# An attention and gated-convolution kernel: q and k loaded alike for both row groups, v issued sooner, reciprocal broadcasts and the first normalisations one to two steps later

## The chip, the cores and the metric

The kernel runs on one core of a Trainium2 chip. The metric is the device time of one execution in microseconds; three runs of the kernel before gave 496.06 us as median (496.01 to 496.46).

## The reference

For four batches of 576 tokens and eight heads of width 64, `q` and `k` are rotated, and softmax attention is computed per head. The heads of a token are laid side by side (512 wide), go through a 512 to 1024 matrix with a ReLU, a convolution of three taps along the tokens, a sigmoid gate, and a 1024 to 512 matrix.

```python
def rotate(x):                      # cos, sin: 576 x 32
    x1, x2 = (x[..., :half], x[..., half:])
    return np.concatenate([x1 * cos - x2 * sin, x1 * sin + x2 * cos], axis=-1)
scores = scale * np.matmul(rotate(q), rotate(k).transpose(0, 1, 3, 2))
attn = np.exp(scores - np.max(scores, axis=-1, keepdims=True))
attn = attn / (np.sum(attn, axis=-1, keepdims=True) + 1e-09)
x = np.matmul(attn, v)              # heads side by side: (4, 576, 512)
h = np.maximum(x @ w_in, 0.0)
conv_out[:, t] = sum(conv_w[k] * h[:, t + k - 1] for k in range(3))
out = (h * sigmoid(conv_out)) @ w_out
```

The weights arrive as 64-bit floats and are turned into 32-bit ones on the chip.

## The kernel before

The work is cut into 16 pairs of heads, p = 0 to 15 (four per batch), and each pair into five steps of 128 query rows (the last has 64). Step number m = 5p + s sets nearly everything: a table `plan` holds for each step a list of pieces with a rank, and `emit` writes the pieces out in order of step and rank. The engines get their instructions in just that order, and each engine runs its own in order, so an instruction that waits holds up all behind it on its engine.

For a pair the pieces are these. `load` (L141 to L151) brings q or k from memory, two heads, in blocks of 32 tokens, into one buffer each (`rq`, `rk`). Each head fills two groups of 32 partitions: the first group gets the row of 64 numbers as it is, in one transfer; the second gets it with its halves swapped, in two. `rope` (L186) rotates on GpSimd (POOL) by six multiplications with the table `tabt` and three additions; `emit_TQ` (L230) turns the result on VectorE (DVE) into `qT` or `kT`, from where TensorE (PE) reads it. `emit_S` makes the scores on TensorE (`sp`), the maxima on VectorE (`negm`) and the exponentials on ScalarE (`st`, and `sums`). `emit_T` transposes them on TensorE (`tp`), ScalarE copies them to `pt`. `emit_E` (L382) multiplies by v (`vm`, `vr`) into `xn`. `emit_rinv` (L363) makes the reciprocals of the sums, writes them to memory in four small transfers (`rd`), and reads them back in three transfers, spread over 64 partitions each (`rb`). The function `norm` (L401) multiplies `xn` by `rb`, and for the first blocks the result goes by DMA to `xT` (L413).

Up to step 25 the kernel is in its first phase, which also converts the weights (`wt`, `wf`: four VectorE instructions a piece, L593 to L609). From step 26 (`WIDE`) on, the two big matrices (`emit_M1`, which reads `xT`, L443; `emit_M2`, `m2_half`) run beside the attention of later pairs, and after the last pair alone.

What matters for the loads: `rq` and `rk` have one buffer each, so the load of pair p waits for `emit_TQ` of pair p - 1. All loads but a few at the start are issued by SyncE (SP), whose queue also holds `rd`, `rb`, `xT`, the loads of v and of the weights (L629), and copies of converted weights (`winl`, L662). Eight completion counters go round, so that a transfer on this queue can be issued only when the one that used its counter last has landed.

Of the kernel before, what the change touches and what calls it, by code (L numbers as in the profile page):

```python
# [20 lines left out]
def attention_moe_kernel(ctx, tc, q, k, v, w_in, conv_w, w_out, tab, tabx, out):  # L21
    nc = tc.nc
# [119 lines left out]
    def load(p, part):  # L142
        b, hp = divmod(p, NPB)
        x = raw[p, part] = p1.tile([128, S // 32, 2, 32], F32, tag="r" + part, name="r" + part)
        for h in range(2):
            y = (q if part == "q" else k)[b, 2 * hp + h].rearrange("(c i) d -> i c d", i=32)
            r0 = slice(64 * h, 64 * h + 32)
            r1 = slice(64 * h + 32, 64 * h + 64)
            nc.sync.dma_start(out=x[r0].rearrange("i c e d -> i c (e d)"), in_=y)
            nc.sync.dma_start(out=x[r1, :, 0, :], in_=y[:, :, 32:64])  # L150
            nc.sync.dma_start(out=x[r1, :, 1, :], in_=y[:, :, 0:32])  # L151

    vmain = {}

    def load_v(p):
        if p < 2:
            nc.vector.memset(vrem[p], 0.0)
        b, hp = divmod(p, NPB)
        t = vmain[p] = p1.tile([128, 2, 4, D], F32, tag="vm", name="vm", bufs=2)
        for h in range(2):  # L160
            nc.sync.dma_start(out=t[:, h], in_=v[b, 2 * hp + h, 0:512, :].rearrange("(t p) d -> p t d", p=128))
            nc.sync.dma_start(out=vrem[p % 2][64 * h:64 * h + 64, h, :], in_=v[b, 2 * hp + h, 512:S, :])
# [23 lines left out]
    def rope(p, part):  # L186
        x = raw[p, part]
        for a in range(0, 18, 3):
            y = x[:, a:a + 3]
            nc.gpsimd.tensor_tensor(out=y, in0=y, in1=tabt[:, a:a + 3], op=ALU.mult)  # L190
        for a in range(0, 18, 6):
            y = x[:, a:a + 6]
            nc.gpsimd.tensor_tensor(out=y[:, :, 0, :], in0=y[:, :, 0, :], in1=y[:, :, 1, :], op=ALU.add)
# [36 lines left out]
    def emit_TQ(p, part):  # L230
        qk_tiles(p)
        x = raw.pop((p, part))[:, :, 0, :]
        if part == "q":
            nc.vector.transpose(out=QT[p].rearrange("p (c i) -> p c i", i=32), in_=x)
        else:
            kt = KT[p].rearrange("p (c i) -> p c i", i=32)
            nc.vector.transpose(out=kt[:, 2:20], in_=x)  # L237
            if p * STEPS < WIDE:
                for h in range(2):
                    r = slice(64 * h, 64 * h + 64)  # L240
                    nc.vector.transpose(out=krem[p % 2][r, r].rearrange("p (c i) -> p c i", i=32), in_=x[r, 16:18])
            if p * STEPS + STEPS > WIDE:
                nc.vector.transpose(out=kt[:, 0:2], in_=x[:, 16:18])
# [6 lines left out]
    def go(d, key):  # L250
        for fn in d.pop(key):
            fn()
# [106 lines left out]
            at(late["n"], 5 if late["n"] > WIDE else 11, lambda dst=dst[:, i], ps=ps: evac("A", dst, ps))  # L359

    rb = {}

    def emit_rinv(p):  # L363
        rv = rvc[p % 2]
        rt = p1.tile([128, 32], F32, tag="rt", name="rt")
        nc.vector.tensor_scalar(out=rv[:, 0:9], in0=sums[p], scalar1=1e-9, scalar2=None, op0=ALU.add)
        nc.vector.reciprocal(out=rv[:, 0:9], in_=rv[:, 0:9])
        nc.vector.transpose(out=rt, in_=rv)
        d = scr.tile([9, 128], F32, tag="d", name="rd")
        for i in range(0, 128, 32):  # L370
            nc.sync.dma_start(out=d[:, i:i + 32], in_=rt[i:i + 9, :])
        fl = d.rearrange("(o t) n -> o (t n)", o=1)
        rbt = rb[p] = p1.tile([128, S], F32, tag="rb", name="rb")
        nc.sync.dma_start(out=rbt[0:64, :], in_=fl[:, 0:S].to_broadcast([64, S]))
        nc.sync.dma_start(out=rbt[64:128, 0:512], in_=fl[:, 640:1152].to_broadcast([64, 512]))
        nc.sync.dma_start(out=rbt[64:128, 512:S], in_=fl[:, 576:640].to_broadcast([64, 64]))
# [330 lines left out]
    WIDE = 26  # L707
    UNITS = {n: 1 for n in (26, 27, 28, 29, 31, 32, 33, 34)}
    UNITS.update({n: 2 for n in (36, 38, 41, 43, 46, 48, 51, 53, 56, 58, 61, 63, 66, 69, 71, 74, 77, 79)})
    HALVES = [37, 39, 42, 44, 47, 49, 52, 54, 57, 59, 62, 64, 67, 68, 72, 73, 76, 78]  # L710
    NORM = {4: 8}
    SPLIT = (38, 39, 42, 43, 44, 45, 47, 48)
    LATEW = (
# [8 lines left out]
    def at(n, rank, fn):  # L722
        plan.setdefault(n, []).append((rank, len(plan.get(n, [])), fn))

    def emit():
        with tc.manual_schedule(engines=engines):
# [6 lines left out]
            for part in "qrk":  # L733
                emit_TQ0(part)
            nc.sync.dma_start(out=tabt, in_=tabx.rearrange("p (c e d) -> p c e d", e=2, d=32))
            load(1, "q")
            load_w(0)
            emit_S(0, 0)
            load(1, "k")
            load_w(1)  # L740
            load_v(0)
# [3 lines left out]
            for p in range(1, NP):  # L745
                n = STEPS * p
                early = n - 10 >= WIDE - 1
                for i, part in enumerate("qk"):
                    if p > 1:
                        at(max(n - 10, WIDE) if early else n - 9 + 2 * i, 19.6 if early else 19, lambda p=p, part=part: load(p, part))  # L750
                    at(n - 8 + i if early else max(n - 6, 0), 18, lambda p=p, part=part: rope(p, part))
                    at(n - 5 + i * (n - 15 < WIDE) if early else max(n - 4 + 2 * i, 2), 0.45, lambda p=p, part=part: emit_TQ(p, part))
                at(n + 1, 19, lambda p=p: load_v(p))
            for p in range(NP):
                n = STEPS * p
                for s in range(STEPS):
                    m = n + s
                    first = m < WIDE
                    if m:
                        at(m - 1 if first else m, 0.5 if first else 0, lambda p=p, s=s: emit_S(p, s))  # L760
                    at(m, 0.2, lambda p=p, s=s: go(reds, (p, s)))
                    at(m, 0.3 if first else 1.5, lambda p=p, s=s: go(exps, (p, s)))
                    for h in range(2 if s < 4 else 1):
                        at(m + 1, 0 if m + 1 < WIDE else 1, lambda p=p, s=s, h=h: emit_T(p, s, h))
                if n + 4 < WIDE:
                    for i in range(4):
                        at(n + 1 + i, 2, lambda p=p, i=i: emit_Trem(p, i))
                else:
                    for i in range(4):
                        at(n + 1 + i, 1.1, lambda p=p, i=i: emit_Trem(p, i))  # L770
                if n + 8 < WIDE:
                    for i in range(4):
                        at(n + 5 + i, 4, lambda p=p, i=i: emit_E(p, i // 2, XW // 2 * (i % 2), XW // 2))
                else:
                    for i in range(2):
                        m = n + 5 + (i if n + 5 < WIDE else 0)
                        at(m, 4 if m < WIDE else 10, lambda p=p, i=i: emit_E(p, i))
                at(n + 5, 4.5, lambda p=p: emit_rinv(p))
                for j in range(2):
                    at(n + NORM.get(p, 8 if n + 8 < WIDE else 7) + (j if p <= WIDE // STEPS else 0), 1.7 + j, lambda p=p, j=j: norms.pop((p, j))())  # L780
            whole, done = sum(c for c, _ in wsteps), 0
# [21 lines left out]
            n = -1  # L803
            while any(plan.values()):
# [17 lines left out]
                while plan.get(n):  # L822
                    e = min(plan[n], key=lambda e: e[:2])
# [16 lines left out]
            t = HS * last // 128  # L840
# [11 lines left out]
def _tables(S, D):  # L852
    import numpy as np

    half = D // 2
    inv_freq = 1.0 / 10000.0 ** (np.arange(0, half, dtype=np.float32) / half)
    fr = np.outer(np.arange(S, dtype=np.float32), inv_freq)
    res = []
    for f in (np.cos(fr), np.sin(fr)):
        f = np.asarray(f, np.float32)  # L860
        m = f[:512].reshape(4, 128, 1, half).transpose(1, 0, 2, 3)
        res.append(np.ascontiguousarray(np.broadcast_to(m, (128, 4, 2, half)).reshape(128, 8, half)))
        r = np.concatenate([f[512:], f[512:]], 0).reshape(128, 1, half)
        res.append(np.ascontiguousarray(np.broadcast_to(r, (128, 2, half))))
    parts = [res[0], res[2], res[1], res[3], np.eye(128, dtype=np.float32)]
    root = float(D) ** -0.25
    cs = [(root * np.cos(fr)).astype(np.float32), (root * np.sin(fr)).astype(np.float32)]
    cs = [x.reshape(S // 32, 32, half).transpose(1, 0, 2) for x in cs]
    turned = [np.stack([cs[0], x], axis=2) for x in (-cs[1], cs[1])]
    return {  # L870
        "tab": np.ascontiguousarray(np.concatenate([x.reshape(128, -1) for x in parts], axis=1)),
        "tabx": np.ascontiguousarray(np.concatenate(turned * 2, axis=0).reshape(128, -1)),
    }
# [26 lines left out]
```

## Time and profile before

| What | Value |
|---|---|
| Median of three runs | 496.06 us (496.01 to 496.46) |
| The profiled execution's own time | 498.59 us |
| Span from its first to its last instruction | 496.7 us |
| PE, DVE, ACT, POOL busy | 460.5, 353.7, 328.3, 291.3 us |
| Mean granted TensorE clock | 0.983 |
| DMA read and written | 37.12 and 4.79 MB |

The times of this section's table and of all rows below are of the one profiled execution. A row's "idle" is the engine's idle time just before an instruction, and the name behind the arrow is what ended it, as far as semaphores show it. Busy time of TensorE is no measure of its speed, since matmuls are pipelined and their ends are modelled. The order listings below the diff are the built programs' order on one engine, with no time in them.

### The profile page before, as it was taken

To read this page: it belongs to the slowest core of one execution; us is meant where nothing else is said; L and a number is where in the kernel's file an instruction comes from. 1 tells how busy PE (TensorE), PEld (TensorE's weight loads), DVE (VectorE), ACT (ScalarE), POOL (GpSimd) and SP (SyncE) were. 2 spreads that over 40 slices of the span, in tenths; PEclk is the share of its full clock that TensorE was granted. 3 is DMA by queue.
4 is the path that set the end of the run, shared out by engine and by line. 5 is a ranking of instruction groups with operands and counts; after the bars stand their busy time and mean duration, and the time that the engine had idled before them with its cause. 6 is when DMAs were issued, how large, how long until landed. Compare 5 with 4: busy or idle time off the path is not lost.

```text
span 496.7 us, 12280 instructions
## 1 busy us (share of the span) xinstructions
PE 460.5 (93%) x4508; PEld 355.3 (72%) x4508; DVE 353.7 (71%) x640; ACT 328.3 (66%) x943; POOL 291.3 (59%) x479
## 2 busy tenths in 40 slices
PE   1888878788999999999999999999999999999997
PEld 1355545455667587777778797979797878899986
DVE  5597695886689988667867777777675565467931
ACT  2687675777698878686859696868687763244510
POOL 3846454888579979599593939392921223234520
PEclk9999799798999999999999999999999999999999
DMA  9975869669554353440706161816120200100011
GB/s 188 229 150 168 173 186 208 158 135 171 142 107 89 56 109 60 81 77 34 134 13 131 36 130 37 131 39 118 48 60 13 60 13 24 44 23 21 1 60 47
DMA packets 142863, 46.00 MB, mean 93 GB/s; under 512 B 132412, under 2 KB 136532, under 8 KB 142804
## 3 DMA queue, kind: packets, MB, share of 16 engines
q1 hardware_dynamic: 141460, 44.83, 42.6%
q8 instruction: 36, 0.59, 0.5%
q10 hardware_dynamic: 1344, 0.39, 0.4%
q14 instruction: 23, 0.19, 0.1%
HBM read 37.12 MB, written 4.79 MB: 84 GB/s over the span
## 4 chain that ended last, share of the span: by engine, by line
PE 64%; DVE 8%; DMA 8%; ACT 7%; SPq 7%; POOL 4%; issue 2%; POOLq 0%; DVEq 0%; ACTq 0%
PE mt L544 10%; PE sp L261 10%; PE pm L564 9%; PE pm L389 9%; PE pm L453 9%; PE mt L453 7%; PE tp L321 5%; PE pm L443 3%; ACT st L273 3%; DMA rd<-rt 2%; DVE negm L269 2%; ACT pt L199 2%; DMA rq<-q 2%; POOL rq L190 2%; SPq L150 1%
## 5 line engine op out<-in xcount | busy, mean ns | idle before, releaser
L269 DVE TENSOR_REDUCE negm<-sp 128x1 f32<-128x576 f32 x144 | 102.4, 747 | 31.9 <-PE sp L261 21.2
L273 ACT ACTIVATE st<-sp,negm 128x576 f32<-128x576 f32 x128 | 93.9, 741 | 37.7 <-DVE negm L269 36.6
L261 PE MATMUL sp<-kT,qT 64*128 64x288 f32 (+4 forms) x556 | 100.2, 465 | 3.7 <-DVE kT L237 1.8
L199 ACT ACTIVATE pt<-tp 128x512 f32<-128x512 f32 (+3 forms) x176 | 84.5, 534 | 10.0 <-PE tp L321 9.5
L190 POOL TENSOR_TENSOR rq<-rq,tabt 128x192 f32<-128x192 f32 x90 | 57.5, 673 | 48.1 <-DMA rq<-q 38.9
L473 DVE SCALAR_TENSOR_TENSOR c<-rr,cw,c 128x288 f32<-128x288 f32 x128 | 78.7, 615 | 4.2
L491 POOL TENSOR_TENSOR gm<-c,gm 128x288 fp32r<-128x288 f32 (+4 forms) x72 | 46.0, 644 | 47.8 <-ACT gm L490 45.2
L261 PEld LDWEIGHTS sp<-kT,qT 64*128 64x128 f32 (+1 forms) x556 | 46.6, 178 | 27.7 <-issue 10.3
L190 POOL TENSOR_TENSOR rk<-rk,tabt 128x192 f32<-128x192 f32 x90 | 59.8, 697 | 6.3 <-DMA rk<-k 4.1
L321 PEld LDWEIGHTS tp<-idf,st 64*128 64x128 f32 x1024 | 42.4, 141 | 26.3 <-ACT st L273 13.5
L321 PE MATMUL tp<-idf,st 64*128 64x64 f32 x1024 | 48.5, 229 | 10.8 <-ACT st L273 9.6
L410 POOL TENSOR_TENSOR xT<-xn,xT 128x290 fp32r<-128x290 f32 x24 | 20.1, 839 | 51.9 <-ACT xT L406 51.8
L389 PE MATMUL pm<-pt,vm 128*64 128x290 f32 x368 | 49.8, 411 | 0.4 <-ACT pt L199 0.4
L564 PE MATMUL pm<-wouth,gm 64*128 64x256 f32 x512 | 49.5, 281 | 0.0
L453 PE MATMUL pm<-xT,winh 128*128 128x290 f32 x224 | 47.1, 304 | 0.0
L482 DVE SCALAR_TENSOR_TENSOR c<-c,rr 128x288 f32<-128x288 f32 x64 | 38.4, 621 | 10.8 <-ACT c L479 10.8
L471 DVE TENSOR_SCALAR c<-rr,cw 128x288 f32<-128x288 f32 x56 | 26.1, 466 | 24.0 <-ACT rr L463 21.2
L564 PEld LDWEIGHTS pm<-wouth,gm 64*128 64x128 f32 x512 | 42.9, 185 | 0.0
L564 PE MATMUL pm<-woutl,gm 64*128 64x256 f32 x256 | 39.0, 276 | 0.0
L389 PEld LDWEIGHTS pm<-pt,vm 128*64 128x64 f32 x368 | 25.5, 136 | 17.9 <-ACT pt L199 1.1
L479 ACT ACTIVATE c<-c 128x288 f32<-128x288 f32 x64 | 28.5, 446 | 12.3 <-DVE c L473 12.3
L453 PEld LDWEIGHTS pm<-xT,winh 128*128 128x128 f32 x224 | 35.9, 189 | 0.9
(120 smaller groups left out, 951.4 us busy)
## 6 DMA issues: line engine op xcount, KB each, us to landing
rq<-q SPq DMA_DIRECT2D x30, 144.0 KB
rq<-q SPq DMA_DIRECT2D x60, 72.0 KB
rk<-k SPq DMA_DIRECT2D x30, 144.0 KB
rk<-k SPq DMA_DIRECT2D x60, 72.0 KB
w<-moe_w_in SPq DMA_DIRECT2D x8, 512.0 KB
vm<-v SPq DMA_DIRECT2D x32, 128.0 KB
w<-moe_w_out SPq DMA_DIRECT2D x8, 512.0 KB
rb<-rd SPq DMA_DIRECT2D x16, 144.0 KB
```

The source lines that it names most:

```text
L190: nc.gpsimd.tensor_tensor(out=y, in0=y, in1=tabt[:, a:a + 3], op=ALU.mult)
L199: nc.scalar.activation(out=out, in_=in_, func=AF.Copy, scale=1.0 if sc is None else sc)
L261: nc.tensor.matmul(out=out, lhsT=qt[64 * h:64 * h + 64, c], rhs=kt[64 * h:64 * h + 64, a:a + n], start=True, stop=True)
L269: reds.setdefault((p, s), []).append(lambda: nc.vector.tensor_reduce(out=nm, in_=sc, axis=AX.XY if len(sc.shape) == 3 else AX.X, op=ALU.ma ...
L273: lambda: nc.scalar.activation(out=dst, in_=sc, func=AF.Exp, bias=nm, scale=1.0, accum_out=sm)
L321: nc.tensor.transpose(ps[r][:, 64 * k:64 * k + 64], x[i], idf[i, i])
L389: nc.tensor.matmul(out=xp[64 * h:64 * h + 64, :], lhsT=vmain[p][:, h, i, :] if i < 4 else vrem[p % 2][:, h, :], rhs=pt[:, 2 * i + h if i < ...
L453: nc.tensor.matmul(out=ps[:, 0:XW], lhsT=w[:, kk, fs], rhs=xT[:, xs, e, :], start=(i == 0), stop=(i == n - 1))
L473: nc.vector.scalar_tensor_tensor(out=c, in0=r[:, j + e:j + e + HS], scalar=cw[:, 8 * e + f:8 * e + f + 1], in1=c, op0=ALU.mult, op1=ALU.add,)
L491: nc.gpsimd.tensor_tensor(out=lo, in0=c[:, o:o + n], in1=hi.bitcast(F32), op=ALU.subtract)
L544: nc.tensor.matmul(out=ops[tt][:, 0:width], lhsT=g_tile(tt, f, e), rhs=w[:, f, cols], start=(f == 0 and i == 0), stop=(f == NF - 1 and i = ...
L564: nc.tensor.matmul(out=ps[r][:, 0:256], lhsT=g_tile(tt, f, e)[rows], rhs=w[rows, f, cols], start=(f == 0 and i == 0), stop=(f == NF - 1 an ...
```

## The change

The loads of q and k give the second group of 32 partitions the same row as the first, in one transfer, four transfers a load in place of six with the same bytes; the swap of the halves is put into the table `tabx`, which now has (sin, cos) for the second group where it had (cos, sin). The loads of q and k of the first phase get rank 16 for 19. The load of v moves from step n + 1 to step n - 1 (n = 5p). The reading back of the reciprocals becomes a piece of its own, `emit_rb`, one step after `emit_rinv` in the first phase and behind that step's load. The normalisations move from step n + 8 to n + 10 for pairs 0 to 2 and to n + 9 for pair 3.

```diff
--- before.py
+++ after.py
@@ -144,11 +144,9 @@
         x = raw[p, part] = p1.tile([128, S // 32, 2, 32], F32, tag="r" + part, name="r" + part)
         for h in range(2):
             y = (q if part == "q" else k)[b, 2 * hp + h].rearrange("(c i) d -> i c d", i=32)
-            r0 = slice(64 * h, 64 * h + 32)
-            r1 = slice(64 * h + 32, 64 * h + 64)
-            nc.sync.dma_start(out=x[r0].rearrange("i c e d -> i c (e d)"), in_=y)
-            nc.sync.dma_start(out=x[r1, :, 0, :], in_=y[:, :, 32:64])
-            nc.sync.dma_start(out=x[r1, :, 1, :], in_=y[:, :, 0:32])
+            for g in range(2):
+                r = slice(64 * h + 32 * g, 64 * h + 32 * g + 32)
+                nc.sync.dma_start(out=x[r].rearrange("i c e d -> i c (e d)"), in_=y)
 
     vmain = {}
 
@@ -359,6 +357,7 @@
             at(late["n"], 5 if late["n"] > WIDE else 11, lambda dst=dst[:, i], ps=ps: evac("A", dst, ps))
 
     rb = {}
+    rds = {}
 
     def emit_rinv(p):
         rv = rvc[p % 2]
@@ -369,7 +368,10 @@
         d = scr.tile([9, 128], F32, tag="d", name="rd")
         for i in range(0, 128, 32):
             nc.sync.dma_start(out=d[:, i:i + 32], in_=rt[i:i + 9, :])
-        fl = d.rearrange("(o t) n -> o (t n)", o=1)
+        rds[p] = d
+
+    def emit_rb(p):
+        fl = rds.pop(p).rearrange("(o t) n -> o (t n)", o=1)
         rbt = rb[p] = p1.tile([128, S], F32, tag="rb", name="rb")
         nc.sync.dma_start(out=rbt[0:64, :], in_=fl[:, 0:S].to_broadcast([64, S]))
         nc.sync.dma_start(out=rbt[64:128, 0:512], in_=fl[:, 640:1152].to_broadcast([64, 512]))
@@ -708,7 +710,7 @@
     UNITS = {n: 1 for n in (26, 27, 28, 29, 31, 32, 33, 34)}
     UNITS.update({n: 2 for n in (36, 38, 41, 43, 46, 48, 51, 53, 56, 58, 61, 63, 66, 69, 71, 74, 77, 79)})
     HALVES = [37, 39, 42, 44, 47, 49, 52, 54, 57, 59, 62, 64, 67, 68, 72, 73, 76, 78]
-    NORM = {4: 8}
+    NORM = {0: 10, 1: 10, 2: 10, 3: 9, 4: 8}
     SPLIT = (38, 39, 42, 43, 44, 45, 47, 48)
     LATEW = (
         ((25, 0.4), (26, 0.25), (26, 0.25), (27, 2.6), (27, 2.6)),
@@ -747,10 +749,10 @@
                 early = n - 10 >= WIDE - 1
                 for i, part in enumerate("qk"):
                     if p > 1:
-                        at(max(n - 10, WIDE) if early else n - 9 + 2 * i, 19.6 if early else 19, lambda p=p, part=part: load(p, part))
+                        at(max(n - 10, WIDE) if early else n - 9 + 2 * i, 19.6 if early else 16, lambda p=p, part=part: load(p, part))
                     at(n - 8 + i if early else max(n - 6, 0), 18, lambda p=p, part=part: rope(p, part))
                     at(n - 5 + i * (n - 15 < WIDE) if early else max(n - 4 + 2 * i, 2), 0.45, lambda p=p, part=part: emit_TQ(p, part))
-                at(n + 1, 19, lambda p=p: load_v(p))
+                at(n - 1, 15, lambda p=p: load_v(p))
             for p in range(NP):
                 n = STEPS * p
                 for s in range(STEPS):
@@ -776,6 +778,7 @@
                         m = n + 5 + (i if n + 5 < WIDE else 0)
                         at(m, 4 if m < WIDE else 10, lambda p=p, i=i: emit_E(p, i))
                 at(n + 5, 4.5, lambda p=p: emit_rinv(p))
+                at(n + 5 + (n + 8 < WIDE), 17 if n + 8 < WIDE else 4.6, lambda p=p: emit_rb(p))
                 for j in range(2):
                     at(n + NORM.get(p, 8 if n + 8 < WIDE else 7) + (j if p <= WIDE // STEPS else 0), 1.7 + j, lambda p=p, j=j: norms.pop((p, j))())
             whole, done = sum(c for c, _ in wsteps), 0
@@ -866,7 +869,7 @@
     root = float(D) ** -0.25
     cs = [(root * np.cos(fr)).astype(np.float32), (root * np.sin(fr)).astype(np.float32)]
     cs = [x.reshape(S // 32, 32, half).transpose(1, 0, 2) for x in cs]
-    turned = [np.stack([cs[0], x], axis=2) for x in (-cs[1], cs[1])]
+    turned = [np.stack(x, axis=2) for x in ((cs[0], -cs[1]), (cs[1], cs[0]))]
     return {
         "tab": np.ascontiguousarray(np.concatenate([x.reshape(128, -1) for x in parts], axis=1)),
         "tabx": np.ascontiguousarray(np.concatenate(turned * 2, axis=0).reshape(128, -1)),
```

SyncE's queue in the middle of the first phase, from the weight load ahead of the reciprocals (`rd`, `rb`) of pair 0 to the q load of pair 3 (`rq`). Before:

```order
L629 DMA w_435<-moe_w_in 128x512
L371 DMA rd<-rt 9x32 x4
L374 DMA rb<-rd 64x576
L375 DMA rb<-rd 64x512
L376 DMA rb<-rd 64x64
L662 DMA winl<-wf 128x512
L161 DMA vm<-v 128x4x64
L162 DMA vr_82<-v 64x64
L161 DMA vm<-v 128x4x64
L162 DMA vr_82<-v 64x64
L149 DMA rq<-q 32x18x64
L150 DMA rq<-q 32x18x32
```

The same stretch of SyncE's queue after the change, from the load of v of pair 1:

```order
L159 DMA vm<-v 128x4x64
L160 DMA vr_82<-v 64x64
L159 DMA vm<-v 128x4x64
L160 DMA vr_82<-v 64x64
L664 DMA winl<-wf 128x512
L631 DMA w_433<-moe_w_in 128x512
L370 DMA rd<-rt 9x32 x4
L664 DMA winl<-wf 128x512
L149 DMA rq<-q 32x18x64 x4
L376 DMA rb<-rd 64x576
L377 DMA rb<-rd 64x512
L378 DMA rb<-rd 64x64
```

The q load of pair 3 now stands ahead of the three `rb`, and the load of v ahead of the `rd`.

VectorE from the transpose of k of pair 2 to the maxima of pair 2's first step (`xn` are the normalisations of pair 0). Before:

```order
L237 STREAM_TRANSPOSE kT<-rk 128x576
L241 STREAM_TRANSPOSE kr_89<-rk 64x64 x2
L403 TENSOR_TENSOR xn<-xn,rb 128x290
L269 TENSOR_REDUCE negm<-sp 128x1
L604 SCALAR_TENSOR_TENSOR wt<-w_296,wt 128x512
L609 SCALAR_TENSOR_TENSOR wf<-w_296,wt 128x512
L403 TENSOR_TENSOR xn<-xn,rb 128x290
L269 TENSOR_REDUCE negm<-sp 128x1 x2
```

The same stretch of VectorE after the change, and on to the first normalisation:

```order
L235 STREAM_TRANSPOSE kT<-rk 128x576
L239 STREAM_TRANSPOSE kr_89<-rk 64x64 x2
L267 TENSOR_REDUCE negm<-sp 128x1
L606 SCALAR_TENSOR_TENSOR wt<-w_290,wt 128x512
L611 SCALAR_TENSOR_TENSOR wf<-w_290,wt 128x512
L267 TENSOR_REDUCE negm<-sp 128x1 x2
L595 TENSOR_SCALAR wt<-wt 128x512
L601 TENSOR_SCALAR wt<-wt 128x512
L606 SCALAR_TENSOR_TENSOR wt<-w_371,wt 128x512
L405 TENSOR_TENSOR xn<-xn,rb 128x290
```

The first normalisation has moved behind three sets of maxima; the rest keeps its order.

SyncE's queue where the first phase ends (`xT` are the results of pair 3, which `emit_M1` reads first in step 26; before, both stand here). Before:

```order
L149 DMA rk<-k 32x18x64
L150 DMA rk<-k 32x18x32
L151 DMA rk<-k 32x18x32
L629 DMA w_1498<-moe_w_out 128x512
L413 DMA xT<-xn 128x290 x2
L371 DMA rd<-rt 9x32 x4
L374 DMA rb<-rd 64x576
```

The same place of SyncE's queue after the change:

```order
L149 DMA rk<-k 32x18x64 x4
L631 DMA w_1473<-moe_w_out 128x512
L159 DMA vm<-v 128x4x64
L160 DMA vr_82<-v 64x64
L159 DMA vm<-v 128x4x64
L160 DMA vr_82<-v 64x64
L415 DMA xT<-xn 128x290
L370 DMA rd<-rt 9x32 x4
L376 DMA rb<-rd 64x576
L377 DMA rb<-rd 64x512
L378 DMA rb<-rd 64x64
L415 DMA xT<-xn 128x290
```

The first `xT` of pair 3 now has the load of v ahead of it, and the second stands behind the `rb`.

## Rows read from the trace of the kernel before

**Rows 1.** Windows: length, busy PE, PEld, DVE, ACT, POOL (counts); clock, DMA share, GB/s

```profile
29.40:47.31 17.91, 16.15 (x196) 10.47 (x193) 16.55 (x29) 15.35 (x41) 12.61 (x18) 1.00 0.77 174
47.31:71.44 24.13, 19.09 (x191) 12.20 (x191) 17.25 (x31) 15.66 (x43) 11.88 (x18) 0.86 0.73 172
71.44:96.01 24.57, 18.97 (x191) 12.09 (x193) 18.20 (x36) 14.67 (x40) 13.82 (x23) 0.86 0.89 194
96.01:114.86 18.85, 16.51 (x197) 10.64 (x193) 16.08 (x28) 15.69 (x42) 15.47 (x26) 1.00 0.73 144
114.86:131.00 16.14, 13.88 (x97) 7.79 (x99) 7.77 (x20) 10.22 (x28) 13.11 (x24) 0.89 0.79 169
131.00:497.00 366.00, 360.04 (x3546) 293.80 (x3542) 259.28 (x467) 242.32 (x719) 208.52 (x346) 1.00 0.30 63
```

**Rows 2.** TensorE timeline: start, us, line, operation, count, idle before and its releaser

```profile
51.23 0.80 PE L321 MATMUL tp<-idf,str 64*128 64x64 f32 x10 [2.26 <-ACT str L273]
51.82 2.02 PE L261 MATMUL sp<-kT,qT 64*128 64x512 f32 x4
...
57.65 1.08 PE L261 MATMUL sp<-kT,qT 64*128 64x512 f32 x4
```

**Rows 3.** VectorE timeline: pair 2 and 3 transposes, first normalisation

```profile
38.98 0.77 DVE L234 STREAM_TRANSPOSE qT<-rq 128x576 f32<-128x576 f32 x1
...
46.38 0.78 DVE L237 STREAM_TRANSPOSE kT<-rk 128x576 f32<-128x576 f32 x1 [1.04 <-POOL rk L193]
...
49.18 0.46 DVE L403 TENSOR_TENSOR xn<-xn,rb 128x290 f32<-128x290 f32 x1 [1.64 <-DMA rb<-rd]
...
62.19 0.78 DVE L234 STREAM_TRANSPOSE qT<-rq 128x576 f32<-128x576 f32 x1 [2.69 <-POOL rq L193]
...
85.67 0.78 DVE L234 STREAM_TRANSPOSE qT<-rq 128x576 f32<-128x576 f32 x1 [4.34 <-POOL rq L193]
```

**Rows 4.** Chain of waits, 39 to 61 us: start, us, what

```profile
39.56 5.82 DMA rd<-rt
...
50.46 0.53 SPq L149
...
53.19 2.87 DMA rq<-q
...
56.71 3.80 POOL rq L190 x6
60.51 1.66 POOL rq L193 x3
```

**Rows 5.** GpSimd waits by releaser, 10 to 131 us

```profile
POOL rq L190 <- DMA rq<-q: 35.4, 6, 10.4
```

**Rows 6.** VectorE groups, pairs 1 to 4: count, busy us, mean ns, idle before

```profile
L609 DVE SCALAR_TENSOR_TENSOR wf<-w,wt 128x512 int32<-128x512 int32 x11 | 9.0, 823 | 0.2
L604 DVE SCALAR_TENSOR_TENSOR wt<-w,wt 128x512 int32<-128x512 int32 x11 | 8.4, 767 | 0.2
L593 DVE TENSOR_SCALAR wt<-wt 128x512 f32<-128x512 f32 (+1 forms) x12 | 7.2, 606 | 0.0
L599 DVE TENSOR_SCALAR wt<-wt 128x512 int32<-128x512 int32 (+1 forms) x12 | 7.0, 584 | 0.3
```

**Rows 7.** VectorE timeline: one weight step beside GpSimd work, one without

```profile
64.96 0.70 DVE L599 TENSOR_SCALAR wt<-wt 128x512 int32<-128x512 int32 x1
...
72.74 0.41 DVE L599 TENSOR_SCALAR wt<-wt 128x512 int32<-128x512 int32 x1
```

**Rows 8.** DMA queues, 206 to 213.5 us (q, k loads): packets, MB, share of engines

```profile
q1 hardware_dynamic: 6412, 1.24, 111.5%
```

**Rows 9.** Chain of waits at the change of phase

```profile
122.86 4.12 DMA xT<-xn
```

**Rows 10.** TensorE timeline at the change of phase

```profile
124.54 1.73 PE L443 MATMUL pm<-xT,winl 128*128 128x290 f32 x6
127.03 0.76 PE L443 MATMUL pm<-xT,winl 128*128 128x290 f32 x2 [0.76 <-DMA xT<-xn]
```

## The prediction

> **What bounds the kernel now.** I read the windows first, cut at the first score matrices of pairs 1 to 5, the change of phase, and the rest [rows 1]. In the rest TensorE (PE) is busy for 360.04 of 366.0 us; the change leaves its work there as it is, so that part can hardly shrink. What can move is the first phase. The four stretches of pairs 1 to 4 do nearly the same work, yet take 17.91, 24.13, 24.57 and 18.85 us, 85.46 in all. VectorE (DVE) is busy for 16.55 + 17.25 + 18.20 + 16.08 = 68.08 us of it, more than ScalarE or GpSimd (POOL), and idle for 17.38. In the first stretch it idles for only 1.36. PE's own busy time in the second and third is inflated: the granted clock averages 0.86 there, and after a wait of 2.26 us for exponentials the same four score matmuls take 2.02 us in place of 1.08 [rows 2], which is 1.2 against 2.4 GHz.
>
> Why VectorE idles is in its timeline and the chain of waits. The transposes of q wait for the rotation on GpSimd, 2.69 us for pair 3 and 4.34 for pair 4; the normalisation at 49.18 waits 1.64 us for the broadcast `rb` and holds up the maxima behind it [rows 3]. GpSimd in its turn waits for q loads, 35.4 us in six waits [rows 5]. And these loads are late because SyncE stands still: the chain shows `rd` in flight for 5.82 us up to 45.4, ahead of `rb` on the queue, and the first q load of pair 3 issued at 50.46 [rows 4], though `qT` of pair 2 had freed its buffer at 38.98 + 0.77 = 39.75 [rows 3]. So a loop over SyncE, DMA and GpSimd sets the pace of the second and third stretch; where it doesn't, VectorE does.
>
> **The change, part by part.** *The broadcasts behind the q load.* The load of pair 3 then waits only for its buffer and is issued from about 39.8, 10.7 us sooner, the four issues taking 4 x 0.53 = 2.1 us (0.53 and the landing of 2.87 after the last issue are rows of the chain [rows 4]). The data are there at about 39.8 + 1.6 + 2.9 = 44.3. GpSimd is still at k of pair 2, which it hands over at 46.38 [rows 3]; then the rotation of q (3.80 + 1.66 = 5.46 us [rows 4]) ends near 51.9, where it ended at 62.17. VectorE asks for it at 62.19 - 2.69 = 59.5 on the old clock, some 5 us sooner on the new: the wait is gone with 2 to 3 us to spare. The same holds for k, whose load stands behind that of q on the queue and on GpSimd, and for pairs 4 and 5. Late next are these: one rotation with GpSimd's conversions of w_out ahead of it, or one landing.
>
> *Four transfers for six.* Two issues of 0.53 us fewer per load, 2.1 us a pair on SyncE, hidden in the above. For the DMA engines the pieces per pair fall from 2 x 2 x (576 + 1152) = 6912 to 4608. While such loads run alone, 6412 packets take 111.5% of 7.5 us on 16 engines [rows 8], or 1.115 x 7.5 x 16 / 6412 = 20.9 ns each, short and long mixed. If a packet of 256 bytes costs what one of 128 costs, a pair saves 2304 x 20.9 ns / 16 = 3.0 us; if time goes by bytes, nothing. I take the middle, 1.5, and give it no term of its own: it only keeps transfers from becoming the bound.
>
> *The normalisations later.* The 1.64 us at 49.18, and through it the 2.26 us of TensorE with the slow clock behind, go away; by then `rb` has been under way for four steps. The same instructions run later, so the busy time stays.
>
> *v sooner.* Four issues (2.1 us) move ahead of a pair's `rd` on SyncE. Cost bounded by 0 and 2.1 us for one `rd`, which is no longer waited for by anything urgent; I take 0. If that cover is gone, it is those 2.1 us a pair on the loop.
>
> *What VectorE then does.* Idle left: at best what the first stretch shows beside its wait of 1.04 us for k [rows 3], 1.36 - 1.04 = 0.32 a stretch, 1.3 in all; at worst the fourth stretch's 18.85 - 16.08 = 2.77 each, 11.1 in all. I take 0.32 for the first and about 1.0 (one late hand-over like that 1.04) for each of the others: 3.3.
>
> A dearer VectorE stands against it: one weight step takes 0.70 us while GpSimd rotates and 0.41 while it rests [rows 7]. There are 11 + 11 + 12 + 12 = 46 such steps in the stretches, and the means, 584 ns for that kind, lie between [rows 6]. GpSimd is busy for 12.61 + 11.88 + 13.82 + 15.47 = 53.78 us, 63% of 85.46; in 73 us it is 74%. With 0.29 us between the two, 46 x 0.29 x (0.74 - 0.63) = 1.5 us are added. The bounds are 0 and, if every step ran slow, about 46 x 0.29 x 0.37 = 4.9. The Trainium skill, page "SBUF — State Buffer", section "Who interferes with whom", says that the two engines share one pair of ports and that the lock is exclusive: whichever holds it blocks the other for a whole instruction. By that rule the 0.41 and 0.70 are the two sides of the lock and the worst case is all 46 steps, so the sum would be 3.4 us worse; the trace agrees with a contention but its mean of 584 shows only part of the steps caught.
>
> *The change of phase.* The stretch from 114.86 to 131.0 has a clock of 0.89 [rows 1], 16.14 x 0.11 = 1.8 us lost, which may or may not come back. I take 0.
>
> **The sum.** 68.08 + 1.5 + 3.3 = 72.9 us for the four stretches, against 85.46: 12.5 saved, and what follows moves up by as much, since TensorE has 6 us of idle in the 366 that come after. From the profiled execution's 498.59 this gives 486.1. The median of the three runs is 496.06, 2.5 less than the profiled one; I carry the difference over: 483.6 us.
>
> **The rivals.**
>
> *1. Transfers become the bound.* The share of the DMA engines times the stretches is 13.8 + 17.6 + 21.9 + 13.8 = 67.1 us [rows 1]. With 4 x 1.5 saved, 61.1 have to fit into 72.9, a share of 0.84. For it: the mean so far is 67.1 / 85.46 = 0.785, and the eight counters let a load queue behind a weight of 512 KB. Against: the third stretch reached 0.89. Held at 0.785 the stretches take 77.8 us (7.7 saved) with the saving of packets, and as long as now without it. The middle is 4 us, 492.
>
> *2. The change doesn't do what it says.* The q load stands sooner on the queue, but one of its four waits on a counter for a weight in flight, and GpSimd begins as late as before; or what is won is lost where the second phase waits for something else. Against: the q loads are GpSimd's wait of 35.4 us, the phase after has only those 6 us of TensorE idle, and other counters come free on the way. 496.
>
> *3. Slower: the first big product waits for pair 3.* TensorE runs six matmuls on `xT` at 124.54 and waits 0.76 us for pair 3's [rows 10], which landed 4.12 us after its issue at 122.86 [rows 9]. Now pair 3 is normalised a step later (72.9 / 20 = 3.6 us) and its transfer stands behind the four issues of v as well (2.1 us): 5.7 us more of waiting with all of TensorE's queue behind it, and the slow clock after it, as at 51.82 [rows 2]. At 0.86 over a stretch of 24 us that clock costs 3.4, of which 1.8 are there already: 7.3 us. It makes the kernel slower if the first phase gains less than these 7.3; with rival 1's 4 us the time is 499.4. Against: in the kernel before the two transfers stood behind a k load of six issues, now the first stands behind one of four, and only that first one is needed in step 26.
>
> **How the numbers follow.** Forecast 0.71, with its own range of 479 to 491 (idle left at 1.3 and the clock's 1.8 back: 16.4 saved; idle left at 11.1: 4.8 saved); rival 1 0.16; rival 2 0.07; rival 3 0.06. The range of 477 to 494 takes in the forecast and nearly all of rival 1, and leaves out the other two and the far ends. A measurement of this kernel can tell about 0.2%, 1 us, from no change. Faster by more: 0.71 and nearly all of rival 1, 0.85; within: rival 2 and the tail of 1, 0.08; slower: rival 3 and some of 2, 0.07.
>
> **What would show it.** In the profile after, the first score matrices of pairs 2 to 5 should come some 17 to 19 us apart, with VectorE over 90% busy between them; GpSimd's waits for q should fall from 35.4 us to under 15; no normalisation should wait for `rb`; the granted clock should be 1.00 up to pair 5; and the window after 131 should be the same, shifted. A DMA share stuck near 0.8 with GpSimd waiting for loads speaks for rival 1; a TensorE wait of several us for `xT` at the first big product for rival 3. I am wrong if the stretches of pairs 2 and 3 still take over 22 us.

## The result, and the profile after

The changed kernel takes 483.53 us (median, 482.49 to 483.94) where the kernel before took 496.23 beside it: ratio 0.9741, 95% interval 0.9724 to 0.9758, 12.7 us faster. One of the four runs of undo_norm below, 496.33 us, was in a slower state of the chip and is left out of its figures. The profiled executions lie further apart, 498.59 and 483.36, since the one of before was 2.4 above its median and the one of after is at its own. The same cuts as in [rows 1] (columns as there), the kernel after:

```profile
29.04:46.46 17.42, 16.17 (x196) 10.46 (x194) 16.07 (x29) 14.56 (x39) 12.13 (x18) 1.00 0.98 230
46.46:64.28 17.82, 16.10 (x197) 10.50 (x193) 17.53 (x30) 15.10 (x42) 12.05 (x18) 1.00 0.98 223
64.28:85.18 20.90, 18.09 (x196) 11.39 (x193) 19.46 (x35) 16.07 (x42) 15.44 (x25) 0.92 1.11 222
85.18:103.02 17.84, 16.43 (x196) 10.54 (x193) 17.52 (x29) 15.72 (x42) 17.84 (x29) 1.00 0.84 159
103.02:116.50 13.48, 12.52 (x97) 7.57 (x99) 8.81 (x20) 10.05 (x28) 12.77 (x22) 1.00 0.59 150
116.50:481.40 364.90, 359.93 (x3546) 294.08 (x3542) 259.33 (x467) 242.51 (x719) 208.59 (x342) 1.00 0.32 63
```

The four stretches fall from 85.46 to 73.98 us, 10.0 of these 11.5 us in the second (24.13 to 17.82) and third (24.57 to 20.90). VectorE is now busy for 70.58 us of them, 95%, and idle for 3.4, where it idled for 17.4. The change of phase gives 2.66 more, and the rest is the same, shifted. With 0.36 before the first cut and 0.8 behind the last that is 11.48 + 2.66 + 0.36 + 0.8 = 15.3, the difference of the spans.

VectorE's timeline after, beside [rows 3]: transposes of pairs 2 and 3, first normalisation.

```profile
39.03 0.78 DVE L232 STREAM_TRANSPOSE qT<-rq 128x576 f32<-128x576 f32 x1 [1.03 <-DMA w<-moe_w_in]
...
52.24 0.85 DVE L405 TENSOR_TENSOR xn<-xn,rb 128x290 f32<-128x290 f32 x1
...
55.88 0.77 DVE L232 STREAM_TRANSPOSE qT<-rq 128x576 f32<-128x576 f32 x1
...
63.37 0.76 DVE L235 STREAM_TRANSPOSE kT<-rk 128x576 f32<-128x576 f32 x1
...
75.41 0.41 DVE L405 TENSOR_TENSOR xn<-xn,rb 128x290 f32<-128x290 f32 x1
```

A bracket at the end of a line shows the idle time before it. From 45 us to the end of the first phase at 116.5 no transposition and no normalisation has one, so none waited in this execution; in another one of the same kernel, after_again, one normalisation waits 1.4 us for `rb`. SyncE's queue (start, us, line, count) with one of its waits (in all, times, longest), then GpSimd's timeline and waits of the same kernel say why:

```profile
39.18 1.88 SPq L370 DMA_DIRECT2D rd<-rt  x4
41.10 0.50 SPq L664 DMA_DIRECT2D winl<-wf  x1
41.70 3.12 SPq L149 DMA_DIRECT2D rq<-q  x4
44.92 0.48 SPq L376 DMA_DIRECT2D rb<-rd  x1
```

```profile
SPq L149 <- DMA w<-moe_w_in: 2.0, 2, 1.1
```

```profile
48.61 4.16 POOL L188 TENSOR_TENSOR rq<-rq,tabt 128x192 f32<-128x192 f32 x6 [3.58 <-DMA rq<-q]
52.73 1.90 POOL L191 TENSOR_TENSOR rq<-rq 128x192 f32<-128x192 f32 x3
...
68.53 3.83 POOL L188 TENSOR_TENSOR rq<-rq,tabt 128x192 f32<-128x192 f32 x6 [6.10 <-DMA rq<-q]
```

```profile
POOL rq L188 <- DMA rq<-q: 20.7, 4, 9.3
```

The q load of pair 3 is issued at 41.70 where it was at 50.46 [rows 4], in front of `rb`. The rotation ends at 54.63 where it ended at 62.17, and VectorE asks for it at 55.88. One of the load's four transfers was held up on the queue for 1.1 us until a weight load had landed. GpSimd still waits for q loads, 20.7 us up to 117 against 35.4 up to 131 [rows 5].

Two places where TensorE could wait, in its timeline after:

```profile
79.70 0.78 PE L319 MATMUL tp<-idf,st 64*128 64x64 f32 x15 [1.37 <-DVE cw L689]
80.42 2.19 PE L259 MATMUL sp<-kT,qT 64*64 64x512 f32 x8
...
110.78 2.51 PE L445 MATMUL pm<-xT,winl 128*128 128x290 f32 x8
```

In the third stretch a copy of the convolution's weights (`cw`) holds TensorE for 1.37 us, and the clock averages 0.92 there: the eight score matmuls at 80.42 take 2.19 us, the same ones at 60.87 take 1.19. At the first big product nothing waits for `xT`, where 0.76 us did [rows 10].

### The profile page after: what moved, and what is told of

Read it like the earlier page. It is cut to its first block, busy times and chain, and to the rows that moved or that the text cites. A ratio compares the mean times of both kernels' runs of the same rounds, so it can differ in the third digit from the quotient of the medians.

```text
span 481.4 us, 12193 instructions
## 1 busy us (share of the span) xinstructions
PE 455.0 (95%) x4508; PEld 352.6 (73%) x4508; DVE 357.0 (74%) x640; ACT 328.4 (68%) x943; POOL 294.2 (61%) x479
## 4 chain that ended last, share of the span: by engine, by line
PE 65%; DVE 13%; ACT 8%; DMA 7%; SPq 2%; issue 2%; POOL 2%; DVEq 0%
PE mt L546 10%; PE sp L259 10%; PE pm L391 10%; PE pm L455 9%; PE pm L566 9%; PE mt L455 7%; PE tp L319 4%; DVE negm L267 4%; PE pm L445 4%; ACT st L271 3%; ACT pt L197 2%; DMA rq<-q 2%; DMA rk<-k 2%; SPq L149 2%; DVE c L475 1%
## 5 line engine op out<-in xcount | busy, mean ns | idle before, releaser
L475 DVE SCALAR_TENSOR_TENSOR c<-rr,cw,c 128x288 f32<-128x288 f32 x128 | 79.7, 623 | 4.2
L188 POOL TENSOR_TENSOR rq<-rq,tabt 128x192 f32<-128x192 f32 x90 | 60.7, 708 | 29.8 <-DMA rq<-q 29.8
L188 POOL TENSOR_TENSOR rk<-rk,tabt 128x192 f32<-128x192 f32 x90 | 57.9, 677 | 4.0 <-DMA rk<-k 2.8
L412 POOL TENSOR_TENSOR xT<-xn,xT 128x290 fp32r<-128x290 f32 x24 | 21.4, 892 | 52.6 <-ACT xT L408 52.5
```

The source lines that it names most:

```text
L475: nc.vector.scalar_tensor_tensor(out=c, in0=r[:, j + e:j + e + HS], scalar=cw[:, 8 * e + f:8 * e + f + 1], in1=c, op0=ALU.mult, op1=ALU.add,)
```

## The experiments

Four readings are tested, which the expectations name by letter or in words (other letters are explained where they stand). Q: SyncE's queue, with `rd` ahead of the q load, set the pace before. C: the later normalisations are only the cover for the later `rb`. V: after the change VectorE's own work sets the pace. L, V's rival: the loop over SyncE, DMA and GpSimd still does, with a shorter round. Each kernel was timed beside the kernel before on one chip. Medians of before were 498.53, 499.93 and 497.15 us in the three sets, so ratios are compared. Even these differ between sets: the same two kernels gave 0.9741 at first and 0.9648 and 0.9708 later, the first two with intervals that don't overlap. Differences of under 1% are therefore read inside one set alone. The edits are cut to the lines that matter; `...` marks a gap.

**only_rb**: before, with `rb` behind the q load, for which the loads of q and k get their rank of 16, and nothing else.

```diff
-        fl = d.rearrange("(o t) n -> o (t n)", o=1)
+        rds[p] = d
+
+    def emit_rb(p):
+        fl = rds.pop(p).rearrange("(o t) n -> o (t n)", o=1)
...
-                        at(max(n - 10, WIDE) if early else n - 9 + 2 * i, 19.6 if early else 19, lambda p=p, part=part: load(p, part))
+                        at(max(n - 10, WIDE) if early else n - 9 + 2 * i, 19.6 if early else 16, lambda p=p, part=part: load(p, part))
...
+                at(n + 5 + (n + 8 < WIDE), 17 if n + 8 < WIDE else 4.6, lambda p=p: emit_rb(p))
```

> The kernel before with only the broadcasts of the reciprocals moved one step later and behind that step's q load (rank 16 of the loads with it). Theory Q (SyncE's queue: what stands ahead of the q load sets the pace of pairs 2 to 4): the largest single part, 486 to 490 us, and GpSimd's waits for q fall from 35.4 us to under 25. Rival P (fewer and longer pieces make the DMA engines faster): about 495. Rival N (the normalisation's wait for rb holds up the maxima): 496 to 500, since rb comes later and the normalisation doesn't.

490.89 us, ratio 0.9855 (0.9804 to 0.9905); of the 496.23 us of the first set that is 489.0, within what Q named. Its waits up to the change of phase, one engine after the other:

```profile
POOL rq L190 <- DMA rq<-q: 14.9, 4, 6.2
```

```profile
DVE xn L407 <- DMA rb<-rd: 6.1, 2, 3.3
```

```profile
PE tp L321 <- ACT str L273: 10.1, 5, 4.0
```

The wait for q falls to 14.9 us, as Q has it. Part of it moves on, since GpSimd now waits some 12 us in front of k, by its waits for a copy of converted weights (5.8), `rd` (4.5) and k (2.0), where before it waited 4.1 us for k up to 117. And the normalisations, still at their old step, now wait 6.1 us for `rb` where they waited 1.6, and TensorE waits behind them.

**only_loads**: before, with the four transfers alone. **only_v**: before, with v sooner alone. **only_norm**: before, with the later normalisations alone.

```diff
-            r0 = slice(64 * h, 64 * h + 32)
-            r1 = slice(64 * h + 32, 64 * h + 64)
-            nc.sync.dma_start(out=x[r0].rearrange("i c e d -> i c (e d)"), in_=y)
-            nc.sync.dma_start(out=x[r1, :, 0, :], in_=y[:, :, 32:64])
-            nc.sync.dma_start(out=x[r1, :, 1, :], in_=y[:, :, 0:32])
+            for g in range(2):
+                r = slice(64 * h + 32 * g, 64 * h + 32 * g + 32)
+                nc.sync.dma_start(out=x[r].rearrange("i c e d -> i c (e d)"), in_=y)
...
-    turned = [np.stack([cs[0], x], axis=2) for x in (-cs[1], cs[1])]
+    turned = [np.stack(x, axis=2) for x in ((cs[0], -cs[1]), (cs[1], cs[0]))]
```

```diff
-                at(n + 1, 19, lambda p=p: load_v(p))
+                at(n - 1, 15, lambda p=p: load_v(p))
```

```diff
-    NORM = {4: 8}
+    NORM = {0: 10, 1: 10, 2: 10, 3: 9, 4: 8}
```

> The kernel before with only the loads of q and k in four transfers for six, and the table to match. Theory Q: two issues of 0.53 us fewer per load on a loop that sets the pace, 2 us a pair over two to three pairs: 490 to 493. Rival P: most of the gain, 484 to 488. Rival N: 496.

> The kernel before with only the load of v two steps sooner (and its rank 15 for 19). Theory Q: four issues less between rb and the q load, 2 us a pair, partly eaten by rd standing behind them: 492 to 495. Rivals P and N: 496.

> The kernel before with only the normalisations of pairs 0 to 3 one or two steps later. Theory Q: only the wait of 1.64 us at pair 2 and the slow clock behind it go, 493 to 495. Rival N: half of the gain or more, 486 to 490. Rival P: 496.

492.15, 495.96 and 499.51 us; ratios 0.9874 (0.9819 to 0.9929), 0.9956 (0.9932 to 0.9981) and 1.0026 (0.9991 to 1.006). The transfers give more than a cover would, while GpSimd's wait for q stays at 32.3 us. The later normalisations alone give nothing, which neither Q (493 to 495) nor N (486 to 490) named; P's 496 fits, but P fails in only_loads, where it named 484 to 488. They give nothing though they take the 1.64 us for `rb` away: VectorE then waits 11.4 us in two waits for the rotation of q. GpSimd's wait in only_loads and VectorE's in only_norm:

```profile
POOL rq L188 <- DMA rq<-q: 32.3, 5, 10.8
```

```profile
DVE qT L234 <- POOL rq L193: 11.4, 2, 7.1
```

At the first big product of only_norm, TensorE's timeline:

```profile
128.00 1.33 PE L443 MATMUL pm<-xT,winl 128*128 128x290 f32 x2 [2.29 <-DMA xT<-xn]
```

**undo_rb, undo_loads, undo_norm**: after, without one part each. In undo_rb the q and k loads have their old rank too.

```diff
-        rds[p] = d
-
-    def emit_rb(p):
-        fl = rds.pop(p).rearrange("(o t) n -> o (t n)", o=1)
+        fl = d.rearrange("(o t) n -> o (t n)", o=1)
...
-                        at(max(n - 10, WIDE) if early else n - 9 + 2 * i, 19.6 if early else 16, lambda p=p, part=part: load(p, part))
+                        at(max(n - 10, WIDE) if early else n - 9 + 2 * i, 19.6 if early else 19, lambda p=p, part=part: load(p, part))
...
-                at(n + 5 + (n + 8 < WIDE), 17 if n + 8 < WIDE else 4.6, lambda p=p: emit_rb(p))
```

```diff
-            for g in range(2):
...
+            nc.sync.dma_start(out=x[r1, :, 0, :], in_=y[:, :, 32:64])
+            nc.sync.dma_start(out=x[r1, :, 1, :], in_=y[:, :, 0:32])
...
-    turned = [np.stack(x, axis=2) for x in ((cs[0], -cs[1]), (cs[1], cs[0]))]
+    turned = [np.stack([cs[0], x], axis=2) for x in (-cs[1], cs[1])]
```

```diff
-    NORM = {0: 10, 1: 10, 2: 10, 3: 9, 4: 8}
+    NORM = {4: 8}
```

> The changed kernel with the broadcasts back with the reciprocals, ahead of the q load, and the loads at rank 19. If the parts add up (alone a ratio of 0.9855), 0.986 to 0.990; theory V, by which shorter loads and v out of the way leave enough room for the wait on rd: 0.977 to 0.983.

> The changed kernel with six transfers a load again. If the parts add up (loads alone gave a ratio of 0.987), 0.985 to 0.988. If instead VectorE sets the pace once the broadcasts are out of the way (theory V), the shorter loads are mostly cover and the ratio is 0.976 to 0.981. In the trace theory V has VectorE over 93% busy between the first score matrices of pairs 2 to 5, adding up has GpSimd wait for q loads some 8 us more.

> The changed kernel with the normalisations back at step n + 8. Alone, moving them gave nothing (499.5 against 498.5). Theory C (cover): they have to move because the broadcasts now come a step later, so here VectorE waits for rb before the maxima in each of pairs 0 to 3: 1 to 2 us a pair, ratio 0.977 to 0.984. Rival F (they are free): the ratio of the changed kernel, 0.973 to 0.975.

490.52, 492.67 and 485.65 us; ratios 0.9828 (0.9771 to 0.9885), 0.9885 (0.9815 to 0.9955) and 0.9728 (0.966 to 0.9796). The whole change, run again beside them:

> The changed kernel once more, as the yardstick for the three beside it: a ratio to the kernel before of 0.974, as measured at first.

481.0 us, 0.9648 (0.9586 to 0.9709). So without the moved `rb` 9.5 us are lost, without the four transfers 11.7, without the later normalisations 4.65. The last is less sure: the two intervals overlap, though each of its three runs (484.55 to 485.93) is slower than each of the four of the whole change (480.08 to 483.38).

The ratios that the expectations name were reckoned from 0.974 for the whole change, and as they stand undo_rb falls into the range of V (0.977 to 0.983) and undo_norm next to that of F (0.973 to 0.975). Beside the 0.9648 of this set the losses are 0.018 and 0.008, and 0.024 for undo_loads. Against 0.974 the expectations come to losses of 0.012 to 0.016 (adding up) or 0.003 to 0.009 (V) for undo_rb, 0.011 to 0.014 or 0.002 to 0.007 for undo_loads, and 0.003 to 0.010 (C) or about 0 (F) for undo_norm. So the first two speak for parts that add up, and more, and the third for C.

In undo_rb the second and third stretch (columns of [rows 1]; 24.13 and 24.57 us before), and what VectorE waits for, are again nearly as before the change:

```profile
46.03:68.38 22.35, 17.88 (x190) 11.21 (x191) 17.21 (x31) 15.34 (x43) 11.86 (x18) 0.92 0.79 182
68.38:91.91 23.53, 18.08 (x191) 11.55 (x193) 17.66 (x35) 15.65 (x41) 14.72 (x25) 0.85 0.88 199
```

```profile
DVE qT L232 <- POOL rq L191: 8.6, 2, 4.3
```

In undo_loads GpSimd waits for k, which stands behind the longer q load on the queue, for 13.3 us, where after it waits 2.2; and the first big product waits too (GpSimd's waits, then TensorE's timeline):

```profile
POOL rq L190 <- DMA rq<-q: 20.0, 4, 7.3
POOL rk L190 <- DMA rk<-k: 13.3, 5, 6.2
```

```profile
122.73 1.33 PE L447 MATMUL pm<-xT,winl 128*128 128x290 f32 x2 [3.31 <-DMA xT<-xn]
```

In undo_norm VectorE's waits name `rb` once more, as C has it:

```profile
DVE xn L405 <- DMA rb<-rd: 4.7, 2, 2.5
```

**no_clamp**: after, without one of VectorE's four instructions per weight piece. It leaves out the bounds for tiny and huge weights in the conversion.

```diff
-            nc.vector.tensor_scalar(
-                out=t.bitcast(F32), in0=t.bitcast(F32), scalar1=bits(F32_TINY), scalar2=bits(F32_HUGE),
-                op0=ALU.max, op1=ALU.min,
-            )
+            return
```

> The changed kernel without the clamp of the weights' absolute values (L595), one of four VectorE steps a weight piece: 11 or 12 steps of 0.61 us fewer in the stretches of pairs 1 to 4, 7 us less work there and a few us more in the weight steps ahead of and behind them (16 pieces and the taps in all); it leaves out the bound for tiny and huge weights. Theory V (VectorE sets the pace of the first phase now): 5 to 8 us faster than the changed kernel, its four stretches together at 67 to 69 us in place of 74. Rival L (the loop over SyncE, DMA and GpSimd still does, at a shorter round): 0 to 1.5 us, with VectorE under 90% busy and GpSimd's waits unchanged.

482.82 us, 0.9699 (0.9659 to 0.9739); the whole change beside it:

> The changed kernel as the yardstick for the two beside it that start from it: a ratio to the kernel before of 0.965 to 0.974.

483.42 us, 0.9708 (0.9659 to 0.9756). The difference of 0.6 us is within the intervals and well under V's 5 to 8 us. The four stretches of no_clamp, then what VectorE and GpSimd wait for up to 117 us:

```profile
28.73:45.38 16.65, 15.93 (x198) 10.39 (x194) 14.16 (x25) 14.46 (x39) 11.96 (x18) 1.00 1.04 231
45.38:63.43 18.05, 16.08 (x197) 10.48 (x193) 14.74 (x26) 16.37 (x44) 11.40 (x18) 1.00 0.84 202
63.43:85.63 22.20, 17.91 (x192) 11.63 (x192) 16.83 (x32) 15.49 (x41) 12.75 (x21) 0.92 0.94 191
85.63:102.87 17.24, 16.21 (x191) 10.53 (x191) 16.80 (x27) 14.33 (x39) 16.33 (x27) 1.00 0.91 175
```

```profile
DVE kT L235 <- POOL rk L191: 3.7, 2, 2.1
DVE negm L267 <- PE sp L391: 3.4, 5, 1.0
DVE xn L405 <- DMA rb<-rd: 2.5, 1, 2.5
```

```profile
POOL rq L188 <- DMA rq<-q: 19.9, 4, 7.2
POOL rk L188 <- DMA rk<-k: 4.1, 2, 4.0
```

VectorE has 62.53 us of work in place of 70.58, and the stretches take 74.14 us in place of 73.98 (73.86 in after_again, 72.49 in after_third). The 8 us come back as idle time, of which these are the largest waits that after doesn't have, while GpSimd's wait for q loads is nearly the same as in after. V falls. L agrees with what was measured, VectorE's busy share of 84% and the unchanged waits included, but no run changes the loop alone and so shows it.

**no_clamp_before**: the same edit on the kernel before.

> The same edit on the kernel before. If the loop over SyncE, DMA and GpSimd set the pace of pairs 2 and 3 there (theory Q), less VectorE work buys little: 0 to 3 us, in pairs 1 and 4 alone. If VectorE's work set it there too, 5 to 8 us.

495.28 us, 0.9979 (0.9947 to 1.0011): nothing to be told from no change, as Q has it. VectorE waits 14.2 us for the rotation of q:

```profile
DVE qT L234 <- POOL rq L193: 14.2, 3, 6.0
```

**cw_spare**: after, with the small transposition for `cw` in a spare buffer and its copy put later, so that TensorE needn't wait 1.37 us.

```diff
-        ps = t_tile()
-        nc.tensor.transpose(ps[:, 0:32], stage.pop("cwf"), idf[0:32, 0:32])
-        nc.vector.tensor_copy(cw, ps[:, 0:32])
+        ps = spare(32)
+        nc.tensor.transpose(ps, stage.pop("cwf"), idf[0:32, 0:32])
+        after(lambda: nc.vector.tensor_copy(cw, ps))
```

> The changed kernel with the transposed taps (cw) put in a free corner of the score bank and copied out a step later, in place of a bank of the transposes. In the changed kernel TensorE waits 1.37 us for that copy at 79.7 and runs at the slow clock after it (stretch of pair 3: 20.9 us, clock 0.92). Theory T (that wait and the clock cost the stretch): 1 to 3 us faster than the changed kernel, clock 1.00 there. Rival V (VectorE sets the pace, TensorE only follows): under 1 us.

484.1 us, 0.9725 (0.9683 to 0.9767): no gain. That wait is gone, but in the same stretch TensorE, by its timeline, now waits longer for k, and the clock averages 0.92 as it did:

```profile
87.28 1.13 PE L259 MATMUL sp<-kT,qT 64*128 64x512 f32 x4 [2.27 <-DVE kT L235]
```

So the price of the slow clock was not tested. That the wait for `cw` brings it isn't so in every execution: in after_third TensorE waits 1.3 us for `cw` as well, and the third stretch runs at full clock, in 19.45 us:

```profile
63.68:83.13 19.45, 16.55 (x192) 10.74 (x193) 18.63 (x34) 15.53 (x42) 13.72 (x21) 1.00 1.08 219
```

No kernel tried here beats the changed one by more than the intervals.

## Why the prediction was right, and where it was off

**The stall on SyncE: right.** The place (stretches 2 and 3) and the mechanism are shown: moving `rb` alone gives 0.9855, and moving it back gives nearly the old stretches (22.35 and 23.53 us). The data came 4.3 us later than reckoned (48.6 for 44.3). The four issues of `rd` still stand ahead of the load (1.88 us of the trace, which the step left out), its own issues took 3.12 us in place of 2.1, 1.1 of it the wait for a weight load, and the rest passed behind the last issue. The rotation so ended 1.25 us ahead of its use and not 2 to 3, and GpSimd's waits for q are 20.7 us and not under 15. Two more of the signs named were missed in one stretch of the four: the third takes 20.90 us, not 17 to 19, at a clock of 0.92, not 1.00.

**The sum: right in total, its terms less so.** VectorE's busy time and idle are 70.58 + 3.4 = 73.98 us, by the prediction 69.6 + 3.3 = 72.9. Of the 2.5 us by which VectorE became dearer, only 0.7 are in the weight steps that the 1.5 was worked out for. VectorE's groups in the four stretches, after:

```profile
L611 DVE SCALAR_TENSOR_TENSOR wf<-w,wt 128x512 int32<-128x512 int32 x11 | 9.4, 857 | 0.2
L606 DVE SCALAR_TENSOR_TENSOR wt<-w,wt 128x512 int32<-128x512 int32 x11 | 8.9, 814 | 0.2
L601 DVE TENSOR_SCALAR wt<-wt 128x512 int32<-128x512 int32 (+1 forms) x12 | 7.3, 606 | 0.3
L595 DVE TENSOR_SCALAR wt<-wt 128x512 f32<-128x512 f32 (+1 forms) x12 | 6.7, 567 | 0.0
L405 DVE TENSOR_TENSOR xn<-xn,rb 128x290 f32<-128x290 f32 x6 | 4.2, 704 | 0.1
...
L365 DVE TENSOR_SCALAR rvc<-sums 128x9 f32<-128x9 f32 x4 | 2.2, 559 | 0.0
```

and of those before the two that grew most:

```profile
L403 DVE TENSOR_TENSOR xn<-xn,rb 128x290 f32<-128x290 f32 x6 | 3.1, 512 | 2.7 <-DMA rb<-rd 1.6 <-DMA rq<-q 0.9
...
L366 DVE TENSOR_SCALAR rvc<-sums 128x9 f32<-128x9 f32 x4 | 1.4, 360 | 0.0
```

The weight steps are 32.3 us against 31.6 [rows 6], so 0.7 more, far from the 4.9 of the worst case. The sums' instruction (`rvc`) costs 0.8 more, for a reason not looked into. The normalisations cost 1.1 more: they moved to where GpSimd rotates (0.85 us at 52.24, inside the rotation of 48.61 to 54.63), and the one at 75.41, with GpSimd between two rotations, takes 0.41.

**"Where it doesn't, VectorE does": wrong.** The sum treats VectorE as what is left to set the pace. It is 95% busy, but no_clamp shows that 8 us less of its work buy nothing clear of noise. That fits a loop and VectorE that stand nearly level after the change, which is argued and not shown. The prediction let the loop drop out, so it is luck that the idle came to 3.4 us beside its 3.3.

**Four transfers for six as a cover without a term: mis-sized.** Alone they give 0.9874, and the change without them is 11.7 us slower, the largest of the three parts undone. Two issues fewer per load shorten the loop itself, since the k load stands behind them. SyncE's timelines agree with that: in undo_loads it issues one transfer after the other from 46.92 to 109.15 us with a single pause of over 0.3 us (0.52). Before, the long pauses are those for `rd` (5.57, 2.09, 2.25 and 1.18 us). The 1.5 us a pair on the DMA engines, on the other hand, are not seen. The main queue in the four stretches (packets, MB, share of 16 engines), before, after and in only_loads:

```profile
q1 hardware_dynamic: 36498, 14.62, 77.8%
```

```profile
q1 hardware_dynamic: 28890, 15.34, 97.5%
```

```profile
q1 hardware_dynamic: 26722, 14.40, 78.9%
```

The share went up to 0.975, not to 0.84: 0.778 x 85.46 = 66.5 us of packet time before and 0.975 x 73.98 = 72.1 after, for 5% more bytes in 21% fewer packets.

**The normalisations: right as a cover, wrong as a gain.** Alone they are worth nothing (1.0026), so the 1.64 and 2.26 us are no gain of their own: the next wait, for q, took their place. They are needed once `rb` comes later (waits of 6.1 and 4.7 us for it in only_rb and undo_norm).

**v sooner: a little more than the 0 taken**, 0.9956 alone. It wasn't undone in the changed kernel.

**The change of phase: 2.66 us where 0 was taken.** The clock is 1.00 where it was 0.89, which is the 1.8 of the forecast's own range; the 0.76 us for `xT` went as well. Which of the parts did it isn't shown.

**The rivals.** The third didn't occur: the first product doesn't wait at all. Its mechanism is real, though: 2.29 us in only_norm and 3.31 in undo_loads, yet neither kernel is shown to be slower than before. The second's mechanism did occur, at a size that its 496 us don't fit: one of the four q transfers waited 1.1 us for a weight load. Of the first, the transfers may well be near the bound now, but no run took bytes away. What sets the loop's round stays open. The traces point to SyncE's own issuing, about 0.5 us for most transfers and up to 3.2 for some: in no_clamp, from 45.38 to 102.47 us, it pauses for over 0.3 us only once (0.51), and in the changed kernel twice from 46.46 to 89.18 (0.52 and 0.39). In the changed kernel's fourth stretch it does pause, and GpSimd is busy for all 17.84 us. Whether the issues are long in themselves or held up by the DMA engines isn't shown, since no run moved transfers to another queue.

**The median.** The profiled forecast was 486.1 and the profiled run took 483.36. The 2.5 us carried over from the profiled run to the median weren't there after; they nearly cancel the change of phase. The time's agreement to 0.1 us, 483.6 against 483.53, is luck to that extent. Nor can 1 us be told from no change, as the prediction took from three runs: before lay between 493.95 and 501.25 us in the later sets.

## What to carry to other kernels

On a queue that issues in order, a transfer that waits for a round trip through memory belongs behind the loads that others wait for, and what reads its result has to move by as much, or it waits in their place. The parts of such a change are to be judged by undoing each, too: one that is worthless alone can be what lets another one pay. An engine that is busy 95% of the time isn't shown to be the bound until some of its work is taken away.

## What was not expected of the hardware

The time of a DMA packet rose from 0.778 x 85.46 x 16 / 36498 = 29.1 ns to 0.975 x 73.98 x 16 / 28890 = 39.9 ns, while the mean packet grew from 401 to 531 bytes. So the packets' time went with the bytes (72.8 and 75.2 us of one engine for each MB), and fewer, longer packets saved none of it. In only_loads, where nothing but the loads is changed, it is 0.789 x 82.17 x 16 / 14.40 = 72.0 us for each MB with 27% fewer packets than before. The share of the engines even stands at 1.11 in one stretch, so packets' times overlap and this view alone doesn't tell when the engines are full.
